# Last batch's attention output: scaled into tiles of 128 tokens and turned by the DMA crossbar, under a new written order

## The chip, the cores and the metric

The kernel runs on one core of a Trainium2 chip. The time is that of one execution on the device, in microseconds (us); where several runs are given, it is their median. The profile is that of one further execution, recorded instruction by instruction. The engines are named as the profile names them: PE is the matrix engine (TensorE), with PEld for its weight loads; DVE is VectorE; ACT is ScalarE; POOL is GpSimd; SP is the queue from which plain DMAs and DMA transposes are issued. SBUF is the on-chip memory, PSUM the eight banks into which PE writes its products.

## The reference, cut to what matters

Attention over 4 batches of 8 heads, 768 tokens and 64 channels a head, in which a query sees the 8 first ("global") keys and the last 96 keys up to itself, with a slope per head on the distance. Its output, 768 x 512 a batch, goes through a gated long convolution:

```python
scores = scale * np.matmul(q, k.transpose(0, 1, 3, 2)) - slopes * dist      # masked by keep
keep = (pos[None, :] < 8) | ((rel >= 0) & (rel < 96))
a = np.exp(scores - max);  a = a / (np.sum(a, -1, keepdims=True) + 1e-09)
x = np.matmul(a, v)                            # -> (B, 768, 512), heads side by side
x1, x2, x3 = split(x @ w_proj, 3)              # 512 columns each
x2_conv = np.fft.irfft(np.fft.rfft(x2, axis=1) * np.fft.rfft(filter_fft, axis=0), n=768, axis=1)
out = (x1 * x2_conv * x3) @ w_out
```

## The kernel before, in words

**Tiling of the attention.** The keys are cut into seven tiles of 128 rows: the 8 global keys and 120 further ones, `KL = 120` apart. For key tile m the scores are computed for a window of up to 216 queries that begins at query 120 m; the widths are in `EW`. The scores of a pair of heads (`hp`, four pairs) and of a group of key tiles (`GRP`: tiles 0-1, 2-3, 4-6) fill two PSUM banks (line 758), ScalarE takes the exponential into the tile `E` (line 773), and VectorE multiplies by a table `mask` made of the distances (line 785). The table `dg` from which `mask` is made is built at the start by POOL (`first`, lines 588 to 595) and by fills on VectorE or ScalarE (`second`, lines 603 to 606).

**Attention output.** `values(j, c, slot)` works on one half of the head pairs (`j`) and one group of tiles (`c`). Output tile t holds 128 queries from 120 t on, so neighbouring output tiles overlap by 8 tokens; it sums key tile t (line 808) and key tile t - 1 (line 813). `v` carries a column of ones, so column 65 of each product is the softmax's denominator. VectorE takes its reciprocal (line 837, `rc`), and the products are scaled into `xn` either by one VectorE instruction (line 832) or by one ScalarE instruction per head and tile (line 836).

**Turning.** The convolution wants channels on the partitions. `transpose_x` turns each 128 x 128 piece of `xn` by a product with the identity on PE (line 853), and a copy (line 313) takes the bank into `xT`, 480 or 576 columns wide, dropping the overlap.

**What reads xT.** The gates (line 931) compute `x1` and `x3` from `xT` and the weights `w`, for the first half (`s = 0`, tokens 0 to 383) and the second (`s = 1`) apart. `butterfly` (lines 867 to 887, VectorE) folds all of `xT` into sums and differences; `proj` (line 992, PE) projects these; then come forward transforms (line 1124), products with the filter's spectrum (lines 1131 to 1152, VectorE), inverse transforms (lines 1022 to 1029), `mixed` (lines 1088 to 1094, VectorE), `half` and the product with the gate (lines 1108 to 1113), and the output projection (line 1058), whose result ScalarE scales into `ot` (line 317) and SP stores (line 1070).

**Staging.** The attention of batch b + 1 stands beside the convolution of batch b. In the last batch (`CROSS = (3,)`) q and k are loaded as token tiles and turned by DMA transposes on SP (line 405: 13 of them, 128 x 512 each), while in the other batches PE turns them. The gates of the last batch are left for the end, where they stand between the dependent steps of the last convolution.

**What sets the order.** No scheduler runs at build time. The string `ORDER` lists every operation by its number in the graph, with the letter of its engine (P, A, V, G for POOL, S for SP) and the PSUM banks that it takes; `i3b7` is a warm-up of three products into bank 7. Each engine carries out its operations in the order of the string, and waits by semaphore where data or a bank is not ready. Where an operation allows it, the letter chooses between ScalarE and VectorE.

## Time and profile before

| what | value |
|---|---|
| time, 3 runs | 165.74 us median (164.07 to 165.93) |
| profiled execution, its own time | 165.28 us |
| its span, first to last instruction | 163.5 us |
| PE busy | 154.6 us, 95% |
| DVE busy | 149.3 us, 91% |
| ACT busy | 150.8 us, 92% |
| POOL busy | 76.9 us, 47% |
| mean granted PE clock | 0.998 |

The span is shorter than the profiled execution's own time by 1.8 us, which lie before the first and behind the last instruction of the program. Busy time is the time in which an engine carries out an instruction. Matmuls are pipelined, so that the mean duration of one (193 ns for a product with 65 columns) is longer than the distance between two of them.

### The profile page before, as it was taken

How to read it: one execution, taken by the hardware profiler on the slowest of the kernel's cores; microseconds unless marked ns; L12 is line 12 of the kernel's file. 1: busy time of each engine (PE TensorE's matmuls, PEld its weight loads, DVE VectorE, ACT ScalarE, POOL GpSimd, SP SyncE). 2: the span in 40 equal slices, each digit the busy share in tenths (PEclk: the TensorE clock that was granted, in tenths of full speed). 3: DMA queues.
4: the chain of work that ended last, by engine and by line, in shares of the span. 5: the costliest groups of instructions: out<-in, count | busy, mean ns of one | idle time of the engine just before them, and what ended most of it. 6: DMA issues, size and time to landing. Idle time of an engine off the chain costs nothing.

```text
span 163.5 us, 4267 instructions
## 1 busy us (share of the span) xinstructions
PE 154.6 (95%) x1607; PEld 94.9 (58%) x1607; DVE 149.3 (91%) x333; ACT 150.8 (92%) x323; POOL 76.9 (47%) x101
## 2 busy tenths in 40 slices
PE   7878989999999999999999999699999999999991
PEld 2355337865656966765667674345657754584540
DVE  6878897899999999999999999879999999999951
ACT  8979999999999999999999999889999988989671
POOL 7999399999994999997880000000000000000000
PEclk9999999999999999999999999999999999999999
DMA  4999999999999999999999964556101530001386
GB/s 120 254 171 180 155 154 177 169 169 183 167 153 136 81 122 136 139 132 172 163 135 156 119 112 107 112 128 149 47 0 67 198 128 0 0 4 56 139 339 238
DMA packets 85036, 21.95 MB, mean 134 GB/s; under 512 B 75664, under 2 KB 82072, under 8 KB 85016
## 3 DMA queue, kind: packets, MB, share of 16 engines
q0 software_dynamic: 73040, 12.11, 99.2%
q1 hardware_dynamic: 11976, 9.57, 22.2%
q8 instruction: 12, 0.20, 0.5%
q14 instruction: 8, 0.07, 0.1%
HBM read 25.40 MB, written 6.29 MB: 194 GB/s over the span
## 4 chain that ended last, share of the span: by engine, by line
PE 79%; ACT 9%; DMA 5%; issue 2%; POOL 1%; DVE 1%; SPq 1%; POOLq 0%; DVEq 0%
PE bank L931 24%; PE bank L992 13%; PE bank L1058 12%; ACT E L773 5%; PE bank L758 5%; PE bank L853 4%; PE bank L808 4%; PE bank L706 3%; DMA kn<-in_k_dram 3%; PE bank L813 3%; PE bank L1022 3%; PE bank L1124 3%; DMA QT<-qn 2%; PE bank L1029 1%; PE bank L689 1%
## 5 line engine op out<-in xcount | busy, mean ns | idle before, releaser
L931 PE MATMUL bank<-xT,w 128*128 128x384 f16 x256 | 48.1, 326 | 0.0
L773 ACT ACTIVATE E<-bank 128x864 f16<-128x864 f32 x48 | 41.0, 913 | 0.8 <-PE bank L758 0.7
L931 PEld LDWEIGHTS <-w 128*128 128x128 f16 x256 | 23.9, 98 | 16.4 <-issue 0.9
L338 POOL DMA_DIRECT2D vn<-in_v_dram x28 | 26.3, 959 | 2.6 <-PE bank L1124 2.1
L338 POOL DMA_DIRECT2D qn<-in_q_dram x25 | 21.7, 873 | 3.5 <-PE bank L758 2.7
L1058 PE MATMUL bank<-wo,y 128*128 128x512 f16 (+1 forms) x100 | 23.0, 370 | 0.0
L338 POOL DMA_DIRECT2D kn<-in_k_dram x25 | 22.0, 891 | 1.9 <-DMA wo<-in_moe_w_out_dram 1.6
L785 DVE TENSOR_TENSOR E<-E,mask 128x1728 f16<-128x1728 f16 x18 | 18.4, 1043 | 0.0
L317 ACT ACTIVATE ot<-bank 128x512 f32<-128x512 f32 (+1 forms) x24 | 14.5, 617 | 2.6 <-PE bank L1058 2.4
L992 PE MATMUL bank<-w,xs 128*128 128x512 f16 x64 | 15.6, 379 | 0.0
L317 ACT ACTIVATE x<-bank 128x384 f16<-128x384 f32 x30 | 15.4, 548 | 0.2 <-PE bank L931 0.2
L808 PE MATMUL bank<-vn,E 128*128 128x65 f16 x224 | 15.4, 193 | 0.0
L313 ACT CAST ab<-bank 128x512 f16<-128x512 f32 x24 | 14.3, 635 | 1.1 <-PE bank L992 1.1
L313 ACT CAST eo<-bank 128x384 f16<-128x384 f32 x31 | 14.2, 532 | 1.2 <-PE bank L1029 1.2
L813 PE MATMUL bank<-vn,E 128*128 128x65 f16 x192 | 15.2, 193 | 0.0
L808 PEld LDWEIGHTS <-E 128*128 128x128 f16 x224 | 14.1, 97 | 1.6 <-issue 0.4
L758 PE MATMUL bank<-QT,KT 64*128 64x216 f16 (+2 forms) x224 | 13.7, 242 | 1.3 <-DMA QT<-qn 1.3
L1058 PEld LDWEIGHTS <-y 128*128 128x128 f16 x100 | 9.4, 98 | 9.2 <-issue 0.4
L313 ACT CAST X<-bank 128x512 f16<-128x512 f32 x24 | 13.8, 633 | 0.9 <-PE bank L1124 0.9
L832 DVE TENSOR_TENSOR xn<-bank,rc 128x512 f16<-128x512 f32 (+1 forms) x19 | 14.5, 772 | 0.2
L758 PEld LDWEIGHTS <-KT 64*128 64x128 f16 x224 | 7.9, 94 | 10.6 <-issue 10.4
L813 PEld LDWEIGHTS <-E 128*128 128x128 f16 x192 | 13.2, 97 | 0.8
(162 smaller groups left out, 334.7 us busy)
## 6 DMA issues: line engine op xcount, KB each, us to landing
out_dram<-ot SPq DMA_DIRECT2D x18, 256.0 KB
vn<-in_v_dram POOLq DMA_DIRECT2D x28, 120.0 KB, 7.1
qn<-in_q_dram POOLq DMA_DIRECT2D x16, 96.0 KB, 5.6
kn<-in_k_dram POOLq DMA_DIRECT2D x16, 96.0 KB, 5.5
out_dram<-ot SPq DMA_DIRECT2D x12, 128.0 KB
w<-in_moe_w_proj_dram POOLq DMA_DIRECT2D x4, 256.0 KB, 6.2
kn<-in_k_dram POOLq DMA_DIRECT2D x7, 120.0 KB, 8.2
g<-in_moe_filter_fft_dram POOLq DMA_DIRECT2D x1, 768.0 KB, 9.3
```

The costliest lines, as they stand in the source:

```text
L313: {"A": nc.scalar.copy, "V": nc.vector.tensor_copy, "G": nc.gpsimd.tensor_copy}[e](out, in_)
L317: self.nc.scalar.mul(out, in_, c)
L338: return self.g.op(eng, 0.57 + 0.00035 * nbytes[0] if eng == "G" else 0.5, lambda _: e.dma_start(dst, src), w=w, r=r, nbytes=nbytes, name= ...
L758: nc.tensor.matmul(bs[hh].f32()[:, off:off + w], self.KT[hs, hp, P * m:P * m + P], self.QT[hs, hp, KL * m:KL * m + w], start=(off == 0 and ...
L773: g.op("A", act(864), lambda _: nc.scalar.activation(eo, bs[0].two()[:, :, 0:432].rearrange("p h (m w) -> p h m w", m=2), Act.Exp, scale=s ...
L785: g.op("V", dve(1728, 2), lambda _: nc.vector.tensor_mul(ep, ep, mk), r=[("mask", h) for h in range(hs.start, hs.stop)], w=[("E", hp - 1, ...
L808: nc.tensor.matmul(o[:, n, hh], ef[:, at:at + P], vt[:, t, 2 * hp + hh, 0:D + 1], start=first, stop=(t == 0), skip_group_check=True)
L813: nc.tensor.matmul(o[:, n, hh], ef[:, at:at + P], vt[:, t - 1, 2 * hp + hh, 0:D + 1], start=False, stop=True, skip_group_check=True)
L832: nc.vector.tensor_mul(to, o[:, :, :, 0:D], rc.to_broadcast([P, 2, 2 * nt, D]))
L931: nc.tensor.matmul(bk.f32()[:, 0:h], self.w[:, c, o + P * j:o + P * j + P], self.xT[:, c, h * s:h * s + h], start=(c == 0), stop=(c == 3))
L992: nc.tensor.matmul(bk.f32(), src[:, c], w[:, c, DM:2 * DM], start=(c == 0), stop=(c == 3))
L1058: nc.tensor.matmul(bk.f32()[:, 0:n], y[:, c, P * t:P * t + P], self.wo[:, c, cs], start=(c == 0), stop=(c == 3))
```

## The change

In the last batch alone (`XCROSS = (3,)`):

- Output tiles are 128 tokens apart and do not overlap: six tiles, grouped as tile 0, tiles 1-2 and tiles 3-5 (`XGRP`). Such a tile takes products from up to three key tiles; a key tile that covers a part of the 128 tokens writes only a run of PSUM partitions that begins at 0, 64 or 96 (`pieces` in the new function `values_x`). A head has 17 products where it had 13.
- The scaled output goes to `xc`, token-major, 128 x 512 for a tile, which lies in the memory of `xn`.
- Six DMA transposes of 128 x 512 on SP (`cross_x`) write `xT` directly. The 28 identity products and the six copies of the last batch go.
- The gates of the second half wait for the last three tiles only, those of the first half for the first three.

In all batches the window of the seventh key tile begins at query 704 instead of 720 (`EQ`), with widths 152 and 64 in place of 168 and 48 for the last two tiles; the table `dg` is built accordingly, with two more fills.

The string `ORDER` is another one throughout, from the first operation on. It also gives other letters to a number of operations in all batches: ScalarE or VectorE for a copy or a scaling. In the built program PE has 1612 products instead of 1607, VectorE 336 instructions instead of 333, ScalarE 335 instead of 321 (its two table loads not counted), and SP issues 62 DMAs instead of 56.

```diff
--- before.py
+++ after.py
@@ -39,54 +39,54 @@
 ORDER = """
-0V 1V 2A 3G 4V 45S 5V 56S i1b7 12P0 34V 17P1 32G 47S 49S 30V 8A 54G 13A 55G 22P2 9V 6V 33V 7G 18A 19A 20V 23A
-51G 14A 46V i3b7 83P3 57A 24A 15V 21A 48V 27V 37V 52G 53G 25V i1b7 81P1 35G 72G i1b7 95P2 39A 50V 38A 84A 31V
...
-976P 969A 964P 970S 977A 965A 971P7 972P 973V 978S 966S 974S
+0V 1V 2A 3G 45S 47S 49S 4V 32G 56S 5V 30A 55G i1b7 12P0 13A 8V 53G 7G 54G 11V 9A 6V 51G 46A 33V 52G 22P1 14V
+34V 17P2 15V 35G 23A 10V 18A 39A 19A 72G 60G 48V 16A i6b7 81P0 38A 24A 61G 20V 37V 62G 50V 41A 25V 21A 82V 44A
...
+968S 970P 964S 971V 972S
 """
@@ -211,7 +211,10 @@
     WL = [], [], [], [(0, 256), (1024, 256), (256, 256), (1280, 256), (512, 512)]
     SHIFT = 0.0
     LONG = 0.6
-    EW = [216, 216, 216, 216, 216, 168, 48]
+    EW = [216, 216, 216, 216, 216, 152, 64]
+    EQ = [KL * t for t in range(6)] + [704]
+    XCROSS = (3,)
+    XGRP = [(0,), (1, 2), (3, 4, 5)]
     GRP = [(0, 1), (2, 3), (4, 5, 6)]
     Q0 = [0, 240, 480]
     QW = [240, 240, 288]
@@ -250,7 +253,10 @@
         self.EE = t("E", [P, 4, 2, 1536])
         self.E = [self.EE[:, i] for i in range(4)]
         self.mask = t("mask", [P, H, 648])
-        self.xn = [t(f"xn{i}", [P, 2, 7, 2, D]) for i in range(2)]
+        xn = t("xn", [P, 4 * 7 * 2 * D])
+        self.xn = [xn[:, 28 * D * i:28 * D * i + 28 * D].rearrange("p (i t h d) -> p i t h d", i=2, t=7, h=2) for i in range(2)]
+        self.xc = xn[:, 0:6 * DM].rearrange("p (t c) -> p t c", t=6)
+        self.xturns = []
         self.xT = t("xT", [P, 4, S])
         self.xab = t("xab", [P, 2, 4, S // 2])
         self.xcf = t("xcf", [P, 4, 4, P])
@@ -400,7 +406,7 @@
                 if not ok:
                     continue
                 gis = [gi for gi, ms in enumerate(self.GRP) if (n in ms if what == "k" else any(
-                    KL * m < P * n + P and KL * m + self.EW[m] > P * n for m in ms))]
+                    self.EQ[m] < P * n + P and self.EQ[m] + self.EW[m] > P * n for m in ms))]
                 out = dst[:, :, P * n:P * n + P]
                 self.g.op("S", 1.3, lambda _, out=out, src=src, n=n: nc.sync.dma_start_transpose(out, src[:, n]),
                           r=[(what + "n", 8 * n + h) for h in range(8)] + ([("kg", 0 if n < 2 else 2)] if what == "k" else []),
@@ -580,31 +586,29 @@
 
 
         g, nc, NL, n = self.g, self.nc, self.NL, 216
-        o = 720 - (self.S - KL)
+        o = 704 - (self.S - KL)
         p, v, dg, far = nc.gpsimd, nc.vector, self.dg, self.far
 
         def first(_):
-            for ap, w, base in ((dg[:, 0:n], n, NG), (dg[:, 600:648], 48, NG + o)):
+            for ap, w, base in ((dg[:, 0:n], n, NG), (dg[:, 584:648], 64, NG + o)):
                 p.iota(ap, pattern=[[-1, w]], base=-base, channel_multiplier=1,
                        allow_small_or_imprecise_dtypes=True)
                 for sgn, off in ((1, 0), (-1, NL - 1)):
-                    if w == 48 and sgn < 0:
-                        continue
                     p.affine_select(ap, ap, pattern=[[sgn, w]], base=off + sgn * base,
                                     channel_multiplier=-sgn, compare_op=Alu.is_ge, fill=-HUGE)
-            p.affine_select(dg[:, 600:648], dg[:, 600:648], pattern=[[0, 48]],
-                            base=-NG - o, channel_multiplier=1, compare_op=Alu.is_ge, fill=-HUGE)
         self.ahead = [g.op("G", 2.0, first, w=["dg"], bias=-9970)]
 
         def second(e):
             put = self.fill if e == "A" else v.memset
             self.copy(e, dg[:, n:2 * n], dg[:, 0:n])
-            self.copy(e, dg[:, 2 * n:2 * n + 168], dg[:, 0:168])
+            self.copy(e, dg[:, 2 * n:2 * n + 152], dg[:, 0:152])
+            put(dg[0:64, 584:632], -HUGE)
+            put(dg[64:NG + 720 - (self.S - KL), 584:632], -HUGE)
             put(dg[0:NG, n:600], -HUGE)
             put(dg[0:NG, n:n + KL], -float(NL))
             put(dg[0:NG, 2 * n:2 * n + KL], -float(NL))
             put(dg[0:NG, 600:648], -float(NL))
-        g.op("AV", {"A": 1.24, "V": 1.24}, second, r=["dg", "idle"], w=["dg2"], name="second", bias=-3500)
+        g.op("AV", {"A": 1.54, "V": 1.54}, second, r=["dg", "idle"], w=["dg2"], name="second", bias=-3500)
         g.op("V", 0.12, lambda _: v.memset(far, 0.0), w=["far"], bias=-3600)
 
         def third(_):
@@ -757,14 +761,14 @@
                     hs = slice(64 * hh, 64 * hh + 64)
                     nc.tensor.matmul(bs[hh].f32()[:, off:off + w],
                                      self.KT[hs, hp, P * m:P * m + P],
-                                     self.QT[hs, hp, KL * m:KL * m + w],
+                                     self.QT[hs, hp, self.EQ[m]:self.EQ[m] + w],
                                      start=(off == 0 and not near), stop=True, skip_group_check=True)
                 off += w
         more = ["dg", "dg1", "dg2", ("slope", 2 * hp), ("slope", 2 * hp + 1)] if near else []
         src = [("QT", hp), ("KT", hp)]
         if self.b in self.CROSS:
-            src = [("kT", m) for m in m0] + [("qT", n) for n in range(KL * m0[0] // P, (
-                KL * m0[-1] + self.EW[m0[-1]] - 1) // P + 1)]
+            src = [("kT", m) for m in m0] + [("qT", n) for n in range(self.EQ[m0[0]] // P, (
+                self.EQ[m0[-1]] + self.EW[m0[-1]] - 1) // P + 1)]
         self.scored[gi].append(g.op("P", 0.65 if near else (0.19 if len(m0) == 2 else 0.2), run, acq=bs, r=src + more,
                                     name="near" if near else "scores"))
         et = self.E[hp]
@@ -839,6 +843,82 @@
         g.op("AV", {"A": 4 * nt * 0.2, "V": dve(4 * nt * D, 1, True)}, scaled, use=bs, r=[key],
              w=[("xn", j, c)], name="xn")
 
+    def values_x(self, j, c, slot):
+        nc, g, D = self.nc, self.g, self.D
+        ts = self.XGRP[c]
+        nt = len(ts)
+        bs = [g.bank(), g.bank()]
+        vt = self.vn[slot]
+        pos = [248 * m for m in range(6)] + [248 * 5 + self.EW[5]]
+
+        def pieces(t):
+            lo, out = P * t, []
+            for m in range(7):
+                a, z = max(lo, self.EQ[m]), min(lo + P, self.EQ[m] + self.EW[m])
+                if a >= z:
+                    continue
+                r0, r1 = (a - lo) // 32 * 32, -(-(z - lo) // 32) * 32
+                r0, r1 = (0, min(96, 248 - lo + self.EQ[m])) if r0 == 0 else (64 if r0 < 96 else 96, P)
+                r1 = P if m == t else r1
+                out.append((m, r0, r1, pos[m] + lo + r0 - self.EQ[m]))
+            return sorted(out, key=lambda x: (x[1] > 0 or x[2] < P, x[0]))
+        parts = [pieces(t) for t in ts]
+        assert all(x[0][1:3] == (0, P) for x in parts)
+
+        def run(_):
+            for low in (0, 64, 96):
+                for i in range(2):
+                    o = bs[i].f32()[:, 0:2 * nt * (D + 1)].rearrange("p (t h d) -> p t h d", h=2, t=nt)
+                    first, hp = not low, 2 * j + i
+                    for hh in range(2):
+                        ef = self.E[hp][:, hh]
+                        for n, part in enumerate(parts):
+                            for m, r0, r1, at in part:
+                                if r0 == low:
+                                    nc.tensor.matmul(o[r0:r1, n, hh], ef[:, at:at + r1 - r0],
+                                                     vt[:, m, 2 * hp + hh, 0:D + 1], start=first, stop=True,
+                                                     skip_group_check=True)
+                                    first = False
+        es = [("E", hp, i) for i in range(max(0, c - 1), c + 1) for hp in (2 * j, 2 * j + 1)]
+        ms = sorted({x[0] for part in parts for x in part})
+        vs = [("vn", slot, m) for m in ms] + [("vn1", slot)] + [("vng", slot, i) for i in range(2) if any(
+            (m >= 2) == bool(i) for m in ms)]
+        g.op("P", 0.03 * 4 * sum(len(x) for x in parts) + (0.19 if c < 2 else 0.28), run, acq=bs, r=es + vs, name="values")
+        rc = self.rc[self.turn % 4][:, 0:4 * nt].rearrange("p (b n o) -> p b n o", b=2, o=1)
+        key = ("rc", self.turn % 4)
+        self.turn += 1
+
+        def view():
+            return bs[0].two()[:, :, 0:2 * nt * (D + 1)].rearrange("p b (n d) -> p b n d", n=2 * nt)
+
+        def scaled(e):
+            o = view()
+            to = self.xc[:, ts[0]:ts[0] + nt, 256 * j:256 * j + 256].rearrange("p t (i h d) -> p t i h d", i=2, h=2)
+            if e == "A":
+                for i in range(2):
+                    for n in range(2 * nt):
+                        nc.scalar.mul(to[:, n // 2, i, n % 2], o[:, i, n, 0:D], rc[:, i, n])
+                return
+            if nt < 3:
+                for n in range(nt):
+                    ns = slice(2 * n, 2 * n + 2)
+                    nc.vector.tensor_mul(to[:, n], o[:, :, ns, 0:D], rc[:, :, ns].to_broadcast([P, 2, 2, D]))
+                return
+            for i in range(2):
+                nc.vector.tensor_mul(to[:, :, i], o[:, i, :, 0:D].rearrange("p (t h) d -> p t h d", h=2),
+                                     rc[:, i].to_broadcast([P, 2 * nt, D]).rearrange("p (t h) d -> p t h d", h=2))
+        g.op("V", 0.066 + 0.025 * nt, lambda _: nc.vector.reciprocal(rc, view()[:, :, :, D:D + 1]),
+             use=bs, w=[key], name="rc")
+        k = nt if nt < 3 else 2
+        g.op("AV", {"A": 4 * nt * 0.2, "V": k * dve(4 * nt * D // k, 1, True)}, scaled, use=bs, r=[key],
+             w=[("xc", j, c)], after=self.xturns, name="xn")
+
+    def cross_x(self, c):
+        for t in self.XGRP[c]:
+            out = self.xT[:, :, P * t:P * t + P]
+            self.g.op("S", 1.3, lambda _, out=out, t=t: self.nc.sync.dma_start_transpose(out, self.xc[:, t]),
+                      r=[("xc", j, c) for j in range(2)], w=[("xT", j, c) for j in range(2)], nbytes=(128, 1024), name="xbar")
+
     def transpose_x(self, j, c):
         nc, g = self.nc, self.g
         ts, W = self.GRP[c], self.QW[c]
@@ -851,7 +931,7 @@
                 for n, t in enumerate(ts):
                     o = step * i + KL * n
                     nc.tensor.transpose(tx[:, o:o + P], self.xn[j][:, i, t], self.ident)
-        g.op("P", 0.0558 * 2 * len(ts), run, acq=[b], r=[("xn", j, c), "ident"], name="trx")
+        self.xturns.append(g.op("P", 0.0558 * 2 * len(ts), run, acq=[b], r=[("xn", j, c), "ident"], name="trx"))
         dst = self.xT[:, 2 * j:2 * j + 2, self.Q0[c]:self.Q0[c] + W]
         g.op("AV", {"A": act(2 * W), "V": dve(2 * W, 2, True)}, lambda e: self.copy(
             e, dst, b.f16()[:, 0:2 * step].rearrange("p (i w) -> p i w", i=2)[:, :, 0:W]), use=[b],
@@ -921,7 +1001,7 @@
     def gate(self, b, j, s):
         nc, g, h = self.nc, self.g, self.S // 2
         gt = self.gt[b % 2]
-        xs = [("xT", i, c) for i in range(2) for c in ((0, 1) if s == 0 else (1, 2))]
+        xs = [("xT", i, c) for i in range(2) for c in ((0, 1) if s == 0 else (2,) if b in self.XCROSS else (1, 2))]
         pts = []
         for o in (0, 2 * self.DM):
             bk = g.bank()
@@ -961,8 +1041,13 @@
             for i in range(4):
                 self.scores(i, c, c < self.NEAR if b == 0 else (i, c) in self.LATER)
             for j in range(2):
+                if b in self.XCROSS:
+                    self.values_x(j, c, b % 2)
+                    continue
                 self.values(j, c, b % 2)
                 self.transpose_x(j, c)
+            if b in self.XCROSS:
+                self.cross_x(c)
             if c:
                 last = b == self.B - 1
                 self.g.bias = 3.0 * self.PERIOD + self.PERIOD * c if last else 0.0
```

92 lines of the change are left out of this document (46 added, 46 removed).

## The prediction

> **What bounds the kernel now.** I read the page's busy times first, then busy time by stretch, then the chain of work that ended last, and then the groups of single lines. By stretch:
>
> ```profile
> core 0: us, PE busy (x) PEld busy (x) DVE busy (x) ACT busy (x) POOL busy (x), PEclk, DMA share, GB/s
> 0.00:26.00 26.00, 22.03 (x215) 10.79 (x216) 20.62 (x77) 23.75 (x49) 21.95 (x38) 1.00 1.48 173
> 26.00:104.00 78.00, 76.68 (x914) 51.54 (x913) 76.55 (x154) 77.06 (x166) 54.99 (x64) 1.00 1.82 143
> 104.00:128.70 24.70, 24.70 (x274) 14.74 (x274) 23.02 (x41) 23.61 (x52) 0.00 (x0) 1.00 0.32 86
> 133.00:160.00 27.00, 26.89 (x176) 14.86 (x173) 24.53 (x58) 22.28 (x49) 0.00 (x0) 1.00 0.26 99
> ```
>
> From 26 us on three engines are full at once: PE for 76.68 of 78 us, VectorE for 76.55, ScalarE for 77.06. None has 2 us to spare, so an engine that gets lighter gains only what the other two allow. The chain names PE for most of the span, with one break:
>
> ```profile
> PE 79%; ACT 9%; DMA 5%; issue 2%; POOL 1%; DVE 1%; SPq 1%; POOLq 0%; DVEq 0%
> ```
>
> ```profile
> 99.92 1.28 SPq L1070
> 101.20 0.05 issue
> 101.29 2.50 DMA QT<-qn
> 103.79 0.14 issue
> 103.93 0.55 PE bank L758 x8
> ...
> 105.44 0.65 PE bank L931 x4
> ...
> 108.77 0.86 PE bank L1058 x4
> ```
>
> The columns are start, length (us) and what the chain passes through. An output DMA stood on SP ahead of a transpose of q, had waited for ScalarE, and PE's scores waited for that transpose. The list of waits gives PE 1.3 us of it:
>
> ```profile
> PE bank L758 <- DMA QT<-qn: 1.3, 1, 1.3
> ```
>
> VectorE's idle time in that stretch (24.70 - 23.02 = 1.7 us) follows from it. What decides the end is the moment at which the last butterfly starts:
>
> ```profile
> 121.83 0.95 DVE L1113 TENSOR_TENSOR y<-y,g 128x1536 f16<-128x1536 f16 x1
> 122.70 1.22 DVE L1142 TENSOR_TENSOR pp<-X,h 128x2048 f16<-128x2048 f16 x1
> 123.83 0.68 DVE L1131 TENSOR_TENSOR p<-X,h 128x1024 f16<-128x1024 f16 x1
> ...
> 128.43 0.42 DVE L1152 TENSOR_TENSOR X<-pp 128x512 f16<-128x512 f16 x1
> 128.77 0.95 DVE L869 TENSOR_TENSOR xab<-xT 128x1536 f16<-128x1536 f16 x1
> ```
>
> It begins as VectorE finishes the instruction before it: `xT` was ready, VectorE was late. From there PE has about 31 us of work and is hardly ever idle (26.89 of 27.00 us). So the end is the butterfly's start plus PE's work behind it.
>
> **The change part by part.** *PE.* Twenty-eight identity products go, 32 products of 65 columns come (136 for 104).
>
> ```profile
> 60.66 1.12 PE bank L853 x20
> 16.29 0.54 PE bank L709 x12
> 123.68 0.19 PE L808 MATMUL bank<-vn,E 128*128 128x65 f16 x1
> 123.71 0.20 PE L813 MATMUL bank<-vn,E 128*128 128x65 f16 x1
> ```
>
> An identity product takes 1.12/20 = 56 ns of PE, a value product 30 ns (one start to the next). So the sum is 32 x 30 - 28 x 56 = 0.96 - 1.57 = -0.6 us. The trace has no product of 65 columns that writes a part of the partitions; 88 of the 136 do (two for each of 8 heads and 6 tiles, less one in tile 0). The nearest are the half-width turns of line 709: 0.54/12 = 45 ns each, with 128 columns. At 45 ns the 88 would cost 1.3 us more, PE +0.7 us; nothing in the trace is shorter than 30 ns, and a gain below that is left out for that reason. I take 30: the 45 ns are for twice as many columns, so the loads of a part of the columns alone need less than that. [...] The 45 ns of line 709 contain such loads of half the columns, so the trace allows no more than that.
>
> *VectorE and ScalarE, last batch.*
>
> ```profile
> L832 DVE TENSOR_TENSOR xn<-bank,rc 128x512 f16<-128x512 f32 x12 | 8.2, 681 | 0.1
> L832 DVE TENSOR_TENSOR xn<-bank,rc 128x768 f16<-128x768 f32 x7 | 6.5, 927 | 0.0
> L945 DVE TENSOR_TENSOR g<-bank,x 128x384 f16<-128x384 f32 x24 | 12.9, 546 | 0.6 <-PE bank L931 0.6
> L836 ACT ACTIVATE xn<-bank,rc 128x64 f16<-128x64 f32 x44 | 9.8, 388 | 0.0
> L313 ACT COPY xT<-bank 128x480 f16<-128x480 f16 x13 | 7.8, 608 | 0.1
> L313 ACT COPY xT<-bank 128x576 f16<-128x576 f16 x6 | 4.2, 706 | 0.2 <-PE bank L853 0.2
> ```
>
> Before, VectorE scaled four of six banks (2 x 0.68 + 2 x 0.93 = 3.2 us); after, one, in two pieces of 128x384, priced like the product of that shape (2 x 0.55 = 1.1): -2.1 us. ScalarE loses six copies (4 x 0.61 + 2 x 0.71 = 3.9 us) and goes from 16 to 36 scalings at 9.8/44 = 0.22 us: +4.5. Net +0.6 us.
>
> *Letters elsewhere.* The new order gives VectorE back what the batch saved. Three more copies into `QT` (0.75 us each) and one more into `xT` (0.40) come to it; a cast, an `eo` copy and an `x1` (0.55 each), four small scalings of `fold` (0.9 together) and, net, one scaling of `xn` (0.4) go; several evictions of tables come. Counted instruction by instruction with the busy time of their groups, this is VectorE +1.7 and ScalarE -2.7 us.
>
> ```profile
> L313 DVE COPY QT<-bank 128x768 f16<-128x768 f16 x6 | 4.4, 748 | 0.4 <-PE bank L709 0.3
> L313 DVE COPY xT<-bank 128x480 f16<-128x480 f16 x3 | 1.2, 396 | 0.0
> L319 DVE TENSOR_SCALAR x<-bank 128x384 f16<-128x384 f32 x2 | 1.1, 552 | 0.3 <-ACT x L317 0.3
> L606 DVE MEMSET eo<- 8x48 bf16 x1 | 0.1, 98 | 0.0
> ```
>
> One gate product (0.55) that stood behind the butterfly now stands ahead of it, and so do two more fills (about 0.1 each, from line 606). Ahead of the butterfly VectorE therefore has -2.1 + 1.7 + 0.55 + 0.2 = +0.4 us. Bounds: +1.4 if the evictions cost what ScalarE's do, -0.6 if the fills and evictions fall into the first 26 us, where VectorE is idle for 26.00 - 20.62 = 5.4 us.
>
> *The transposes and their queue.* Six more stand on SP.
>
> ```profile
> L405 SPq DMA_TRANSPOSE QT<-qn x6: 1192/1222/1977, 79.1 to 101.3; - x6
> L1108 DVE TENSOR_TENSOR y<-eo 128x1024 f16<-128x1024 f16 x6 | 4.0, 672 | 0.0
> ```
>
> SP gives 1.22 us to each (the median), and the chain shows 2.50 us from issue to use, 1.28 beyond the issue. For the last three: 3 x 1.22 + 1.28 = 4.9 us, and the twelve scalings on ScalarE, which must end first, may end 1 us behind VectorE's own two: 5.9 us. Between those two and the butterfly VectorE has, in the new order, two joins (line 1108) with their gate products (line 1113) and all products with the spectrum (lines 1131 to 1152): 2 x 0.67 + 2 x 0.95 + 2 x 0.68 + 2 x 1.22 + 4 x 0.42 = 8.7 us, and some short pieces. So the transposes are hidden with 2.8 us to spare, and I cost them at nothing; without that cover they would cost 5.9. Upper bound: at the slowest issue, 1.98 us, 3 x 1.98 + 1.28 + 1 = 8.2, still inside. The gates that read `xT` sit later still.
>
> On SP the 13 transposes of q and k now all stand ahead of the first output DMA of batch 1, so the break at 99.9 us cannot recur in that form. Next late would be the loads of q and k themselves. Between the first transpose of `xT` and the next stands one pair of output DMAs; its `ot` is scaled on ScalarE ahead of those tiles' own scalings, so it is ready.
>
> *Other queues.* POOL's `first` has as many instructions as before, on 64 columns instead of 48: at most 0.1 us, in the first 4 us. Its loads stand in another sequence, with `wo` last; `wo` is needed only for the first output projection. No load is added.
>
> *Sum.* Butterfly's start: -1.5 for the break (between the 1.3 of the wait and the 1.7 of VectorE's idle time), +0.4 of VectorE. Behind the butterfly's first projection PE has one gate less (4 x 163 ns = 0.65) and one output projection more (0.86): +0.2. Start of the run: up to the first gates both orders ask the same 28.3 us of ScalarE (groups' busy time summed), the engine that is fullest there, and let VectorE begin its first butterfly a little later: +0.2, with 1 us either way as its bounds, from PE's 4 idle us. Sum -0.7: 165.28 - 0.7 = 164.6 us. The median shown, 165.74, is 0.5 above the profiled execution; a gain of 2%, about the least that a measurement of this kernel can tell from no change, would be 162.4.
>
> **The rivals.** *A. PE alone decides.* If VectorE loses its lateness, the whole 0.6 of PE and the 1.5 of the break show: 163.2 us; with the start phase shorter by 1 us, where PE is idle 4 us, 162.2. For it: PE is named 79% of the chain. Against it: the butterfly starts on VectorE's heels.
>
> *B. ScalarE becomes the bound ahead of the butterfly.* From the first scaling of the last batch to its last, the new order gives ScalarE 36 scalings (8.0 us), two exponentials and five copies, 12.0 us by their groups' busy time, and PE beside them six projections, five value groups, two gates and an inverse transform, 10.4 us. A group of twelve holds its banks for 12 x 0.22 = 2.6 us, where VectorE's 0.93 freed them. If PE waits for both, the cost is (12.0 - 10.4) + (2.6 - 0.9) = 3.3 us on top: 167.9 us. For it: ScalarE is full (23.61 of 24.70). Against it: over the whole kernel ScalarE gets 2.1 us lighter.
>
> *C. The crossbar is not covered.* The slower side. It sits between the last scalings and the butterfly and decides from the point at which three transposes take more than the 8.7 us of cover. At 1.22 us apart they do not. If each had to land before the next started, and landed as slowly as a load of like size, it would:
>
> ```profile
> qn<-in_q_dram POOLq DMA_DIRECT2D x16, 96.0 KB, 5.6
> kn<-in_k_dram POOLq DMA_DIRECT2D x7, 120.0 KB, 8.2
> ```
>
> 3 x 5.6 + 1 - 8.7 = 9.1 us: 173.7 us; with the starts overlapped and one landing of 8.2, 2 x 1.22 + 8.2 + 1 - 8.7 = 2.9 us: 167.5 us. Against it stands that the next transpose was issued as the one before it had left SP, after 1.2 us. [...]
>
> *D. Nothing is won.* The order's swaps cancel the gain, and the loads of q are as late as the output DMA was: 164.6 + 1.5 = 166.1 us.
>
> **How the numbers follow.** The forecast, 164.6, gets 0.40, with a range of its own from 163.7 to 165.6 (VectorE's bounds of -1.0 and +1.0 around its +0.4). A gets 0.26, half of it below 162.4; D 0.10; B 0.16, half of it above 169.1 (165.74 and 2%), where PE's upper bound of +1.3 comes on top; C 0.08, most of it above. Faster by over 2%: 0.13, and 0.01 of the forecast's edge: 0.14. Slower by over 2%: 0.08 + 0.07 = 0.15. Within: 0.71. The range runs from 162.0, just below A's low end, to 168.6, which takes in D and B but for B's upper half; outside stand C, that half and what is faster than A, under 0.2.
>
> **What would show it.** Right: no wait of PE for `QT` above 0.5 us; the butterfly's first instruction begins less than 0.2 us behind VectorE's previous one, at about 127.9 us, and the six transposes of `xT` have landed before; value products 30 ns apart; VectorE busy about 150 us. Wrong: VectorE idle ahead of the butterfly with a DMA named (C); PE waiting for ScalarE's `xn` or for banks between 100 and 120 us (B); PE busy for much less or more than 22 us in the first 26.

## The result and the profile after

The changed kernel takes 171.72 us (median; 170.59 to 172.38), the kernel before 165.26 us beside it: 1.039 times as long, 95% interval 1.031 to 1.048. The forecast was 164.6 us, no change. The profiled execution took 170.59 us with a span of 168.8; before it was 165.28 and 163.5. So 5.3 us are to be found. (Line numbers below are each kernel's own: the scores are line 762 in the changed kernel, the gates 1011, the output projection 1143, the value products 878, the butterfly 947.)

The page's chain of work, by engine, of the changed kernel:

```profile
PE 45%; POOL 20%; DMA 18%; ACT 11%; issue 4%; DVE 0%; POOLq 0%; DVEq 0%
```

PE fell from 79% to 45%, and POOL and the DMAs came in, from 1% and 5% to 38% together: the chain now passes through loads. Busy time by stretch, the changed kernel:

```profile
core 0: us, PE busy (x) PEld busy (x) DVE busy (x) ACT busy (x) POOL busy (x), PEclk, DMA share, GB/s
0.00:26.00 26.00, 21.69 (x244) 10.70 (x245) 19.54 (x73) 24.95 (x56) 21.55 (x38) 1.00 1.44 175
26.00:85.00 59.00, 58.70 (x716) 38.98 (x715) 58.01 (x125) 58.35 (x128) 54.86 (x64) 1.00 2.13 146
85.00:95.00 10.00, 6.79 (x85) 4.61 (x84) 9.13 (x15) 6.58 (x15) 0.00 (x0) 1.00 1.71 132
95.00:100.00 5.00, 5.00 (x21) 2.32 (x19) 2.57 (x5) 3.33 (x7) 0.00 (x0) 0.66 1.36 164
104.00:130.00 26.00, 26.00 (x283) 16.43 (x282) 25.00 (x45) 24.24 (x71) 0.00 (x0) 1.00 0.34 73
```

and the kernel before in the same stretches, as far as they differ:

```profile
26.00:85.00 59.00, 58.97 (x728) 39.91 (x726) 57.55 (x121) 58.72 (x120) 54.08 (x63) 1.00 2.01 148
85.00:95.00 10.00, 10.00 (x117) 6.96 (x117) 10.00 (x19) 9.95 (x31) 0.91 (x1) 1.00 1.85 137
100.00:104.00 4.00, 2.71 (x18) 1.16 (x18) 4.00 (x8) 3.55 (x6) 0.00 (x0) 1.00 0.47 105
```

Between 85 and 95 us PE is idle 3.2 us where it was never idle; behind that its granted clock is 0.66 for 5 us (in single microseconds: 0.71, 0.50, 0.50, 0.58). VectorE and ScalarE lose time there too, and ahead of 85 us PE has lost only 0.6 us more than before. The list of waits (who waits, for whom, us in total, times, longest) names the cause:

```profile
ACT E L777 <- PE bank L762: 3.4, 1, 3.4
PEld L762 <- DMA KT<-kn: 3.4, 1, 3.4
DVE g L1025 <- ACT X L319: 3.3, 1, 3.3
PE bank L762 <- DMA KT<-kn: 3.2, 1, 3.2
```

PE waits for the transposed keys of the last batch, and ScalarE and VectorE wait for PE. The chain (start, length, what) and the row of `wo` among the DMAs between 60 and 100 us (KB, median us from issue to landing):

```profile
77.03 7.02 DMA qn<-in_q_dram
84.05 10.10 DMA KT<-kn
94.16 0.05 issue
94.20 0.64 PE bank L762 x10
```

```profile
wo<-in_moe_w_out_dram POOLq DMA_DIRECT2D x1, 512.0 KB, 16.0
```

The transpose of k's second tile took 10.1 us from its issue to its use; the transpose in the broken place of before took 2.50. The loads of v and `wo` were in flight beside it. PE reaches the last batch's first scores at 90.7 us in the new order; in the old one it did at 99.3.

The part that was meant to be the change went as planned. The transposes of `xT`, and VectorE around the butterfly:

```profile
L919 SPq DMA_TRANSPOSE xT<-xn x6: 1190/1204/1912, 116.6 to 127.7; - x6
```

```profile
133.60 0.42 DVE L1237 TENSOR_TENSOR X<-pp 128x512 f16<-128x512 f16 x1
133.93 0.95 DVE L947 TENSOR_TENSOR xab<-xT 128x1536 f16<-128x1536 f16 x1
```

The last transpose leaves SP at about 129 us, and the butterfly begins at 133.93 on VectorE's heels, as before, only 5.2 us later. The value products, from the chain:

```profile
115.89 0.96 PE bank L878 x24
117.82 1.50 PE bank L878 x36
```

A product takes 0.96/24 = 40 and 1.50/36 = 42 ns, not 30. The six groups of the chain add up to 5.62 us for 136 products, 1.5 more than 136 x 30 ns; with the -0.6 of the prediction PE has 0.9 us more to do.

By these rows the 5.3 us are: PE idle between 85 and 104 us 3.2 instead of 1.3 (+1.9), the clock 5 x (1 - 0.66) = 1.7, PE's work +0.9, PE's idle time ahead of 85 us +0.6 (0.34 in the first 26 us, 0.27 behind), in all 5.1. The sum says where the time lies; what it would be worth to take one item away is another question, and the experiments answer it differently for the clock.

### The profile page after: what moved, and what is told of

Its sections match the earlier page's. It is cut to its first block, busy times and chain, and to the rows that moved or that the text cites. A ratio compares the mean times of both kernels' runs of the same rounds, so it can differ in the third digit from the quotient of the medians.

```text
span 168.8 us, 4318 instructions
## 1 busy us (share of the span) xinstructions
PE 157.3 (93%) x1612; PEld 95.0 (56%) x1612; DVE 150.9 (89%) x336; ACT 149.6 (89%) x337; POOL 76.4 (45%) x101
## 4 chain that ended last, share of the span: by engine, by line
PE 45%; POOL 20%; DMA 18%; ACT 11%; issue 4%; DVE 0%; POOLq 0%; DVEq 0%
PE bank L1011 13%; PE bank L1143 12%; DMA qn<-in_q_dram 7%; POOL qn L344 6%; PE bank L1077 6%; DMA KT<-kn 6%; POOL kn L344 6%; POOL vn L344 6%; DMA vn<-in_v_dram 5%; ACT E L777 5%; PE bank L878 3%; PE bank L1107 3%; PE bank L1209 2%; ACT KT L319 2%; PE bank L762 2%
## 5 line engine op out<-in xcount | busy, mean ns | idle before, releaser
L1011 PE MATMUL bank<-xT,w 128*128 128x384 f16 x256 | 50.8, 334 | 0.0
L777 ACT ACTIVATE E<-bank 128x864 f16<-128x864 f32 x48 | 40.3, 934 | 3.5 <-PE bank L762 3.4
L344 POOL DMA_DIRECT2D kn<-in_k_dram x25 | 21.5, 869 | 2.2 <-DVE pp L642 1.0
L762 PE MATMUL bank<-QT,KT 64*128 64x216 f16 (+2 forms) x224 | 14.4, 243 | 3.5 <-DMA KT<-kn 3.2
L1025 DVE TENSOR_TENSOR g<-bank,x 128x384 f16<-128x384 f32 x24 | 12.8, 547 | 5.2 <-ACT X L319 3.3
L319 ACT CAST ab<-bank 128x512 f16<-128x512 f32 x24 | 13.8, 629 | 2.9 <-PE bank L1077 2.9
L323 ACT ACTIVATE ot<-bank 128x512 f32<-128x512 f32 x22 | 12.7, 612 | 4.0 <-PE bank L1143 4.0
L812 PE MATMUL bank<-vn,E 128*128 128x65 f16 x168 | 11.3, 193 | 0.4 <-ACT E L777 0.3
L836 DVE TENSOR_TENSOR xn<-bank,rc 128x512 f16<-128x512 f32 (+1 forms) x14 | 11.1, 794 | 0.2
L817 PE MATMUL bank<-vn,E 128*128 128x65 f16 x144 | 11.2, 193 | 0.0
L812 PEld LDWEIGHTS <-E 128*128 128x128 f16 x168 | 10.4, 97 | 1.1
```

The source lines that it names most:

```text
L319: {"A": nc.scalar.copy, "V": nc.vector.tensor_copy, "G": nc.gpsimd.tensor_copy}[e](out, in_)
L323: self.nc.scalar.mul(out, in_, c)
L344: return self.g.op(eng, 0.57 + 0.00035 * nbytes[0] if eng == "G" else 0.5, lambda _: e.dma_start(dst, src), w=w, r=r, nbytes=nbytes, name= ...
L762: nc.tensor.matmul(bs[hh].f32()[:, off:off + w], self.KT[hs, hp, P * m:P * m + P], self.QT[hs, hp, self.EQ[m]:self.EQ[m] + w], start=(off ...
L777: g.op("A", act(864), lambda _: nc.scalar.activation(eo, bs[0].two()[:, :, 0:432].rearrange("p h (m w) -> p h m w", m=2), Act.Exp, scale=s ...
L812: nc.tensor.matmul(o[:, n, hh], ef[:, at:at + P], vt[:, t, 2 * hp + hh, 0:D + 1], start=first, stop=(t == 0), skip_group_check=True)
```

## The experiments

Two theories at the start. **Loads**: the new order's sequence of loads, transposes and scores makes PE wait, whatever the way of turning. **Crossbar**: the six transposes with their scalings and value products cost the 5 us.

### The new order with the identity products (ident_after)

```diff
-ops 795S 812S 813S 850S 851S 852S (transposes of xT), values of 17 products a head
+ops 792P 797P 812P 817P 852P 857P and their copies, values of 13 products a head, as in before.py
 the rest of the changed ORDER as it is
```

> The changed order with the identity products and their copies back in place of the crossbar (values of 104 products, six groups of turns each behind its own scaling, three of the six copies on VectorE). Two theories of where the 5.3 us between the spans come from. Theory 'loads': the new order asks for the first scores of the last batch at 90.7 us instead of 99.3, while its keys are still on their way; PE waits 3.4 us for KT, then runs five microseconds at a clock of 0.66; the way of turning has nothing to do with it. Then this kernel is as slow as the changed one within 1 us, 170.7 to 172.2, with the same wait for KT. Theory 'crossbar': the six transposes, the 36 scalings on ScalarE and the value products that write a part of the partitions cost the 5 us. Then this kernel comes back to 165 to 167.

Measured: 174.48 us (1.056, 1.047 to 1.065), above the expected range. Its waits, and its stretch behind the wait:

```profile
PE bank L754 <- DMA KT<-kn: 3.1, 2, 2.9
```

```profile
95.00:100.00 5.00, 4.16 (x25) 1.97 (x24) 3.27 (x6) 4.02 (x8) 0.00 (x0) 1.00 1.39 129
112.00:130.00 18.00, 14.66 (x178) 9.03 (x178) 15.97 (x33) 15.29 (x52) 0.00 (x0) 1.00 0.12 29
```

The wait for KT is there without any crossbar, so it belongs to the order. The rest, 3.3 us of PE idle between 112 and 130 us, is new. The list of waits puts most of it on ScalarE's scalings (1.3 and 0.4 us) and on a copy into `xT` (0.6), the rest on a mask product (0.7) and a cast (0.5): the turns need scaling and copy in turn, and this order has too little other work beside them. The theory "crossbar" falls as an account of the wait; what the crossbar costs by itself, this run doesn't tell.

### The loads of v behind wo (v_last)

```diff
-681G 690G 686G 680G 675G 677G 676G 688G 687G 678G 685G 257G
+681G 680G 675G 677G 676G 678G 257G 690G 686G 688G 687G 685G
```

(257 is the load of `wo`, 685 to 690 those of the last batch's v.)

> The changed kernel with five of the last batch's seven loads of v issued behind the load of wo instead of ahead of it; nothing else is moved. The five loads are 0.6 MB, at the 140 GB/s of that stretch 4.3 us. Theory 'loads': keys, queries and wo land up to 4 us earlier, the wait for KT falls from 3.4 us to between 0 and 1.5, the clock keeps 1.00, and the time falls to 167 to 169.5. Theory 'crossbar': 171.7, unchanged. A third reading, that the transposes themselves are slow beside any load (10.1 us for the one that PE waits for, whatever stands behind it): the wait stays within 1 us of 3.4 and the time above 170.5.

Measured: 168.96 us (1.024, 1.014 to 1.034): 2.8 us less than the changed kernel, 2.6 by the two ratios to the kernel before, by the sequence of POOL's loads alone. Of the wait there is left

```profile
PEld L758 <- DMA KT<-kn: 1.7, 2, 1.2
```

and PE loses 2.1 us in three gaps, at 91.0, 96.7 and 97.8 us (the 2.9 us in an expectation below is too much). The clock stays at 1.00. This is what the theory "loads" expected, though the wait did not go.

### One transpose two places later (k1_first)

```diff
-778S 768S 770S
+768S 770S 778S
```

> The changed kernel with one transpose on SP set back by two places: that of k's last tile (needed at 105 us) stood ahead of that of k's second tile (needed at 90.7 us). The second tile's is then issued at 82.0 us instead of 84.05. If its 10.1 us belong to the transpose, it lands at 92.1, PE waits 1.3 us instead of 3.4, and the time is 169 to 170. If the DMA engines' backlog sets the landing, it lands at 94 as before and nothing changes: 171.7 within 0.5. Theory 'crossbar' expects no change either.

Measured: 171.27 us (1.034, 1.023 to 1.045), not told apart from the changed kernel. But the wait for KT is gone. In its place:

```profile
PE bank L1139 <- DMA wo<-in_moe_w_out_dram: 2.7, 1, 2.7
```

```profile
95.00:100.00 5.00, 2.95 (x16) 1.15 (x15) 2.75 (x6) 1.08 (x3) 0.00 (x0) 0.70 1.25 189
```

PE gets past the scores and stops at the first output projection, for `wo`, the last load of all, which landed at 97.0 us. The transpose's place decided which of two late transfers PE met first; none of the expectations had this. PE is busy for the whole of each microsecond from 88 to 94 us and waits for no transpose there; so that of k's second tile had landed by 91 us: within 9 us of the expected issue at 82.0, an estimate from the two, where it had taken 10.1, with the same loads in flight. That speaks for its place behind another transpose as a part of the 10.1 us; how much the loads add is not separated.

### The wait filled with idle products (warm)

```diff
-781P67 782A 641V
+641V i15b3 781P67 782A
```

> The changed kernel with 15 products of 512 columns (216 ns each, 3.2 us in all) that nobody reads, put on PE ahead of the scores that wait for KT; the wait is filled with work and its end, the landing at 94.2 us, is not moved. If PE's idleness is what lowers the granted clock behind the wait (0.66 between 95 and 100 us), the clock stays at 1.00 there and 1.7 us are won: 170.0. If the clock falls for another reason, the time stays at 171.7 or is a little longer.

Measured: 171.68 us (1.036, 1.026 to 1.047), no gain, although the clock stayed:

```profile
95.00:100.00 5.00, 3.83 (x29) 2.26 (x30) 1.44 (x3) 3.35 (x6) 0.00 (x0) 1.00 1.29 187
```

```profile
PE bank L759 <- DMA KT<-kn: 1.5, 1, 1.5
```

In this execution the keys' transpose landed at 96.1 us, 2 later than in the other, so PE still waited 1.5 us. And even with the landing at 94.2 not all of the 1.7 us could have been won: PE came to the projection that needs `wo` at 99.3 us, 0.9 behind `wo`'s landing (82.4 + 16.0). By these figures a full clock would have won 0.9 us, an estimate, and the other 0.8 would have become a wait for `wo`.

### The loads in order of need (v_held, v_held6)

```diff
+        g.op("G", 0.1, lambda _: self.nc.gpsimd.memset(self.kn[:, 2, 0:8], 0.0))
 POOL: keys, queries, wo, then this fill (it waits for the transpose that reads kn), then v
-766S 771S 767S 769S 778S 768S 770S 775S 773S 683S 772S 774S 777S 776S
+766S 771S 767S 769S 768S 770S 773S 775S 683S 772S 774S 777S 776S 778S
```

> The changed kernel with the loads taken in the order of need: the five late loads of v wait on POOL (behind a small fill that waits until the transpose of k's third tile has read its source) instead of standing ahead of wo, and on SP the transposes of k and q stand in the order in which the scores ask for them. With the loads of v alone moved behind wo the time was 168.96 and three waits of PE, 2.9 us together, were left. Theory 'loads': without the loads of v beside them the transposes land in time, the waits go, the clock stays at 1.00: 168.96 - 2.9 = 166.1, between 165.3 and 167. Theory that the transposes are slow for themselves: a wait of 1 us or more stays at the first scores and the time is above 167.5.

Measured: 166.73 us (1.011, 1.006 to 1.015), inside the range of the theory "loads"; no wait is left at the first scores, but one later, for the last tiles of k, whose transposes stand beside the released loads of v:

```profile
PE bank L758 <- DMA KT<-kn: 1.6, 1, 1.6
```

So the fill was made to wait for k's last tile (`kn[:, 6, 0:8]`):

> As the changed kernel with the loads in order of need, but the five loads of v now wait until the transpose of k's last tile has read its source, so that no load stands beside the last transposes; with the earlier release PE still waited 1.9 us at 99.9 for the last tiles of k. Theory 'loads': that wait goes too, 166.7 - 1.5 to 1.9 = 164.8 to 165.2. If the transposes of the last tiles are late for another reason (SP's own 1.25 us each), the wait stays and the time is 166.3 to 166.9.

Measured: 165.54 us (1.008, 1.005 to 1.011). Now PE has no idle time where the changed kernel had 3.2 us:

```profile
90.00:95.00 5.00, 5.00 (x37) 2.61 (x35) 5.00 (x9) 4.73 (x9) 0.00 (x0) 1.00 0.47 92
95.00:100.00 5.00, 5.00 (x48) 2.75 (x49) 5.00 (x10) 5.00 (x9) 2.12 (x4) 1.00 0.25 46
100.00:104.00 4.00, 4.00 (x45) 2.69 (x41) 4.00 (x6) 4.00 (x8) 2.49 (x3) 1.00 1.77 165
```

From the changed kernel's 171.7 to 165.5 are 6.2 us; by the ratios to the kernel before, each taken beside it, the loss falls from 3.9% to 0.8%, which is 5.1 us. They came from the sequence on POOL and SP, with PE's, VectorE's and ScalarE's orders and all of the crossbar path untouched. That is most of the loss, shown. With the loads of v set back, the DMA share between 90 and 95 us is 0.47, where it was 1.62, and no score waits for a transpose. A transpose of k took 10.1 us beside the loads (changed kernel, DMA share 1.71 between 85 and 95 us), one of q 2.50 with few of them (before, 0.47 between 100 and 104 us); how the loads hold a transpose up, no run here shows.

### The price of writing a part of the partitions (wide)

```diff
+                r0, r1 = 0, P
-                out.append((m, r0, r1, pos[m] + lo + r0 - self.EQ[m]))
+                out.append((m, r0, r1, min(max(pos[m] + lo - self.EQ[m], pos[m]), pos[m] + self.EW[m] - P)))
```

> As the kernel with the loads in order of need, but each of the last batch's 136 value products writes all 128 partitions (88 of them wrote 32 to 96). Rows that lie outside a piece are summed in as well, so the attention of the last batch is another one; the number and the kind of all instructions are the same. In the changed kernel's trace a product that writes a part, or stands beside such a one, takes 35 to 41 ns, two full ones in a row 29.5. If it is the part that costs, the 136 take 30 ns each, 1.3 us less than before this edit, and as PE sets the end the time falls by 1.0 to 1.4 us. If it is the number of products or their waits, nothing changes.

Measured: 165.59 us (1.004, 1.002 to 1.007) against 166.73 of v_held, on which it stands: about 1 us, for as many instructions (the output is another one, so this is a test of the price and no kernel to use). The two intervals all but touch; the trace is clearer. A group of 36 value products in the chain of v_held and then of wide:

```profile
114.91 1.50 PE bank L874 x36
116.19 1.09 PE bank L875 x36
```

That is 42 ns a product against 30; the pieces' shape costs that. By the starts of the single products in the changed kernel's trace, the price has two parts. Within a run of products that write from the same first partition, one start follows the other after 28 to 52 ns, mostly 35 to 41, where wide has 30. And at each of the eight places where the first partition changes (0 to 64, 0 to 96, 64 to 96) 120 to 135 ns pass: eight times about 98 ns more than 30 is 0.8 us, half of the 1.5. Whether the change itself takes that was not tested: in wide all products begin at partition 0, and with that their sequence changes too.

### The crossbar in the order of before (before_xbar), and its wait filled (xbar_warm)

```diff
-before.py: 792P 793A 797P 798A 812P 813A 817P 818A 852P 853A 857P 858A
+after.py's values_x and cross_x, each transpose as soon as its scalings end; the other words of before's ORDER in their sequence
```

> The change's way of turning alone: values of six tiles, scaling into tiles of 128 tokens and six transposes on SP, in the order of before (each transpose as soon as its scalings end, every engine's other work in its old sequence; the letters V and A as before). In the trace of before the last scaling of the last batch ends at 126.93 us and the butterfly starts at 128.77. Theory 'loads' with the crossbar at its price: 3 x 1.22 + 1.28 = 4.9 us from that scaling to the butterfly, 3.1 more than before, and 0.7 to 1.3 of PE for the value products: 168 to 169.5, with no wait for KT over 1.5 us and VectorE waiting for xT. Theory 'crossbar' (the path costs some 5 us whatever stands beside it): 170 or more. If the path is free wherever it stands: 164 to 165.5.

Measured: 174.91 us (1.059, 1.053 to 1.066), 5 us above the expected range. VectorE:

```profile
128.88 1.01 DVE L904 TENSOR_TENSOR xn<-bank,rc 128x384 f16<-128x384 f32 x2
...
135.57 0.96 DVE L945 TENSOR_TENSOR xab<-xT 128x1536 f16<-128x1536 f16 x1 [3.75 <-issue]
```

and the busy time by stretch:

```profile
135.00:140.00 5.00, 0.99 (x6) 0.32 (x4) 4.30 (x7) 1.12 (x3) 0.00 (x0) 0.77 0.71 267
140.00:145.00 5.00, 5.00 (x16) 2.05 (x15) 4.60 (x9) 1.95 (x4) 0.00 (x0) 0.54 0.00 0
```

From the end of the last scaling (129.89) to the butterfly 5.7 us pass, close to the 4.9 expected and to the 5.9 that the prediction gave for transposes without cover: the three transposes are issued from 130.42 on, behind two output DMAs on SP, the first takes 1.22 us of SP, and the last is used 5.15 us after the first was issued. What the expectation lacked: the last scaling itself ended 3.0 us later than the 126.93 of before, in a stretch in which VectorE waited 2.1 us for value products and before for none; and behind the butterfly's start 2.9 us more pass than before, in which PE, idle 4 us ahead of the first projection, ran at half clock (0.50 in each microsecond from 138 to 144). So the total lies where the theory "crossbar" had it (170 or more): in an order without cover the path costs 10 us. To see whether the clock is worth its time, PE's wait was filled:

```diff
-882P0
+i18b6 882P0
```

> The kernel with the crossbar in the order of before, where PE stood idle 4.2 us ahead of the first projection of the last butterfly and then had a granted clock of 0.50 for about 6.5 us, with 18 products of 512 columns that nobody reads (216 ns each, 3.9 us) ahead of that projection; VectorE's butterfly, for which PE waits, does not depend on them. If PE's own idleness lowers the clock, it stays at 1.00 behind the wait and half of 6.5 us, 3.2 us, are won: 174.9 - 3.2 = 171.7. If the clock falls for another reason, the time is 174.9 or a little more.

Measured: 174.81 us (1.056, 1.046 to 1.065), the same total. The clock did hold:

```profile
140.00:145.00 5.00, 5.00 (x27) 2.45 (x26) 4.92 (x10) 2.95 (x7) 0.00 (x0) 1.00 0.01 5
```

The filling ran past the end of the wait, so that the first projection began 1.0 us later (140.45 instead of 139.50); even so the gate behind the last projection started 1.5 us earlier (147.80 instead of 149.34). But at the end an output DMA was late instead:

```profile
164.35 4.20 DMA out_dram<-ot
```

So in both pairs the clock went with PE's idleness: it held at 1.00 when the wait was filled, where it had been 0.66 (changed kernel, 95 to 100 us) and 0.54 (before_xbar, 140 to 145 us). That the lower clock lengthened a total by its own amount, neither shows.

### The kernel before, mended (before_fix, before_fix2, before_need)

```diff
-317S 773S 776S 778S 320S
+773S 776S 778S 317S 320S
```

> The kernel before with one output DMA on SP set behind the last transposes of q and k; it stood ahead of three of them, and PE waited 1.3 us for the first of these. If the output DMA was the cause, the wait goes and the time falls by 1.0 to 1.5 us, to 163.3 to 163.8. If the load of q behind it is just as late, or the waiting scores only come to the next limit, it stays at 164.8 within 0.4.

Measured: 163.07 us (0.986, 0.981 to 0.991). The profiled execution does not fit: it took 165.08 us, the other three 162.63 to 163.14, and the wait that was to go is still in it.

```profile
PE bank L755 <- DMA QT<-qn: 1.6, 1, 1.6
```

> The same kernel as before_fix, measured again with more rounds, since its profile still shows PE waiting 1.6 us for QT at 102 us although its time fell by 1.7 us: its transposes took the place of the output DMA. If the output DMA's place is worth something, 163.1 again, 1 to 2 us below the kernel before; if the first measurement was a chance, within 0.5 us of it.

Measured: 162.92 us (0.991, 0.988 to 0.994; the kernel before had 164.35 in this set). In this second profile the wait is all but gone:

```profile
100.00:104.00 4.00, 3.74 (x27) 1.72 (x26) 4.00 (x8) 4.00 (x7) 0.00 (x0) 1.00 0.39 71
```

PE is idle 0.26 us instead of 1.29. One output DMA's place on SP was the break of before. The last run gives this kernel the sequence of need as well:

```diff
+        g.op("G", 0.1, lambda _: self.nc.gpsimd.memset(self.kn[:, 2, 0:8], 0.0),
+             w=[("kn", 8 * 2)])
 POOL: wo, keys and queries, this fill, then v 685G 686G 687G 689G 690G
 SP: 766S 767S 768S 769S 771S 684S 770S 772S 773S 775S 774S 776S 777S 778S 317S
```

> The kernel before, its turning by identity products untouched, with the same change in the sequence of loads and transposes: the last batch's keys and queries are loaded before its v, whose late loads wait on POOL for the transpose of k's third tile, the transposes stand on SP in the order of need, and the output DMA behind them. Theory 'loads': the break of 1.3 to 1.9 us at 102 us goes, 164.9 - 1.5 = 163.4, and with the changed kernel in the same sequence about 165 what is left between them, 1.5 to 2 us, is the price of the crossbar path itself (value products 1.1, the rest its waits). Theory that the sequence is of no use to this order: 164.9 within 0.5.

Measured: 162.82 us (0.991, 0.987 to 0.994), no different from before_fix2, and both ahead of either kernel of the case. The comparison at a like sequence (the loads of v wait for k's last tile there, for its third here) is then 165.54 for the changed kernel (v_held6) and 162.82 here: 2.7 us, 2.3 between the profiled spans (163.6 and 161.3). Page lines and first stretches, v_held6 and then before_need:

```profile
PE 155.8 (95%) x1612; PEld 95.2 (58%) x1612; DVE 150.2 (92%) x336; ACT 149.4 (91%) x337; POOL 76.6 (47%) x102
...
0.00:26.00 26.00, 22.23 (x244) 11.45 (x244) 19.34 (x72) 24.95 (x56) 21.56 (x38) 1.00 1.43 174
26.00:85.00 59.00, 58.70 (x718) 39.04 (x715) 57.94 (x126) 58.56 (x130) 50.38 (x59) 1.00 2.05 151
```

```profile
PE 154.4 (96%) x1607; PEld 95.0 (59%) x1607; DVE 148.6 (92%) x333; ACT 150.7 (93%) x323; POOL 76.9 (48%) x102
...
0.00:26.00 26.00, 22.74 (x238) 11.61 (x239) 21.20 (x79) 24.47 (x50) 21.33 (x38) 1.00 1.46 170
26.00:85.00 59.00, 58.96 (x714) 39.77 (x711) 57.13 (x120) 58.73 (x122) 51.00 (x59) 1.00 2.07 151
```

In v_held6 PE has 1.4 us more work (about 1 of it the pieces' shape) and 0.8 us more idle time ahead of 85 us. The second lies ahead of all that the crossbar path does; whether the new order or the other window of the seventh key tile causes it was not separated. How the order alone would do with whole-width products was not tried in a form that keeps the output.

## Why the prediction was wrong, by its steps

- **What bounds the kernel.** Right in part: the butterfly starts on VectorE's heels in both, and PE's work behind it sets the end. But wide, which shortens only PE's work ahead of the butterfly, was about 1 us faster, so that work counts too, and the sum had no term for it. The output DMA on SP as the cause of the break was right as well: moving that one word won 1.4 to 1.8 us.
- **"The break at 99.9 us cannot recur in that form", and -1.5 for it in the sum.** This is the step that failed. The form was gone, the wait was not: 3.2 us for KT, and 1.7 us of slow clock behind it. The sign asked for, no wait for `QT` above 0.5 us, was there and told nothing. The text named the next limit ("the loads of q and k themselves") and then gave it no time. Two facts in the order bore on it: scores asked for 8.6 us earlier, and five loads of v among the last keys and ahead of `wo`; with the sequence of need the wait was gone.
- **"Its loads stand in another sequence, with wo last; ... No load is added."** Costed at nothing, and wrong for the same reason: what counted here was not the number of loads but what had landed when PE asked. `wo` landed at 98.4 us instead of 77.6; in k1_first PE stood 2.7 us for it. The output projections with `wo`, which the old order had on PE from 91.3 us on, could not start in the new one before 98.4.
- **PE: value products at 30 ns.** Wrong; 41 ns on the mean of all 136: +0.9 us of PE and not -0.6, which is above the upper bound of +0.7 too, since that raised the price of the 88 partial products alone and had nothing for the changes of the first partition. The run with whole-width products shows about 1 us for the shape; why such products take longer, no run shows. The reason given for taking 30 (half the columns need less) does not hold.
- **VectorE about 150 us busy, ScalarE lighter.** 150.9 and 149.6, against 149.3 and 150.8: as said, and neither decided anything.
- **Transposes of xT hidden.** Right; and without cover (before_xbar) 5.7 us pass from the last scaling to the butterfly, for 5.9 given. Rival C did not come to pass.
- **The start, +0.2.** 0.3 in the first 26 us, and 0.3 more up to 85 us that was not seen.
- **Rivals.** D had the mechanism, late loads, with the size of the old break (1.5 us). The wait alone was 3.2, and with it came the clock (0.66 for 5 us). No rival had the slow clock, and none was priced by following the loads' landings against the scores' new place.

## What to carry to other kernels

When an order is rewritten, take each engine's first request for data of the next stage and ask when its last transfer lands in the new sequence of the queues, other queues' loads included; a load that is needed late belongs behind those needed early, even if it must be made to wait. The sequence of DMA issues was worth 5 to 6 us here. The way of turning cost 1 to 2 where the order hid the transposes (2.7 us less the 0.8 of idle time at the start), and 10 in an order that did not. PE, full in the old profile, paid 41 ns for a value product of the new shape where it had paid 30: where an engine is full, bound a new shape of its instruction by the nearest row, let the bound cover the unchanged instructions beside it as well, and take the pessimistic end where there is no cover.

## What was not expected of the hardware

- Behind or within PE waits of 3.2 us (changed kernel), 2.7 (k1_first) and 4.0 (before_xbar) the granted clock fell to 0.50, for 3.4, 3.4 and 6.8 us by the clocks of the single microseconds; after 2.9 us in ident_after it stayed at 1.00. With products that nobody reads in the wait (warm, xbar_warm) it stayed at 1.00 behind it. So the length of the wait alone did not decide it: 2.7 us were enough in one execution, 2.9 were not in another.
- In the changed kernel a product of 65 columns that writes 32 to 96 of the 128 partitions, or stands next to such a one, takes 37 ns on the mean from start to start (28 to 52), whole ones in a row 30 (wide, 1.09/36); where the first partition changes, 120 to 135 ns pass.
- A DMA transpose of 128 x 512 took 2.5 us from issue to use at a DMA share of 0.47 (before, 100 to 104 us) and 10.1 at one of 1.71 (changed kernel, 85 to 95 us), though SP was free of the one after 1.24 us and of the other after 2.21.
